# Forgetting attention and a GELU MLP on one core: key tiles joined on VectorE before the denominators, and the value weighting moved to another stage

## The chip, the cores and the metric

The kernel runs on one core of a Trainium2 chip. A core has five engines that run their own instruction streams: TensorE (PE, with its weight loads shown as PEld), VectorE (DVE), ScalarE (ACT), GpSimd (POOL) and SyncE (SP, here only a queue that issues transfers). GpSimd, SyncE and ScalarE issue DMAs from their own queues. The metric is the device time of one launch in microseconds: the median of the runs. Before the change it is 342.06 us (3 runs, 341.93 to 342.09).

## The reference

Eight batches with eight heads each, a sequence S of 576 and a head dimension of 64, then an MLP over the 4608 rows that the attention gives:

```python
scores = scale * np.matmul(q, k.transpose(0, 1, 3, 2))
cum = np.cumsum(np.log(np.clip(f, 0.0001, 1.0)), axis=-1)
decay = cum[:, :, :, None] - cum[:, :, None, :]
scores = np.where(causal, -1000000000.0, scores + decay)
attn = np.exp(scores - scores.max(axis=-1, keepdims=True))
attn = attn / (attn.sum(axis=-1, keepdims=True) + 1e-09)
x = np.matmul(attn, v)                        # then heads side by side: [4608, 512]
g = gelu_tanh(x @ w_in)                       # 512 -> 2048
out = g @ w_out                               # 2048 -> 512
```

The decay splits into a factor of the query, which cancels in the quotient, and a factor of the key. So with P = exp(scale * k q) under the causal mask and w[key] = exp(-cum[key] - 64), the output is (sum over keys of P w v) / (sum over keys of P w).

## The kernel before, in words

Work goes by quads: quad i is four heads of batch i // 2, so there are 16 quads. Keys lie on the partitions, five key tiles of 128 (the last holds 64). P of a quad is the tile `pt` [128, 4 heads, 1536 columns]; each head's columns are the pieces of L51: "low" (64 columns, the first 64 queries against the first keys), key tile 0 (512 columns), 1 (448), 2 (320), 3 (192) and "high", which shares the first 64 columns with "low" on the other partitions. A later key tile has fewer columns since the causal mask leaves fewer queries.

- `scores` (S, L202) makes P of a quad in three rounds: products on TensorE, exp on ScalarE (L228). `mask` (A in the new table, L230) then clears the triangle on GpSimd (`affine_select`, L234), in part also on VectorE (L263) for the early quads.
- `denominators` (D, L297) is the sum over keys of P w: `product` (L266) runs 24 matmuls, six pieces for four heads, with w as the weights; the four heads run side by side in 128x32 column groups of TensorE, so a piece costs its columns once. The result lies in the one PSUM buffer `psO`. VectorE then transposes, takes reciprocals and transposes back (L307 to L311).
- `attn_out` (V, L315) is the same product with `vw`, v times w, as the weights, for one half x of the head dimension; VectorE multiplies it by the reciprocals into `xT` (L319) and so frees `psO`.
- `make_vw` (VW, L174) computes v times w for a quad: one GpSimd instruction of 1280 elements a partition (L178). `copy_low` (CL, L182) copies a part of it on VectorE.
- `mlp_in` (L322) is the first MLP product for 512 rows (chunk c) with GELU, in eight parts of eight matmuls. `mlp_out` (L357) is the second, 64 units for a chunk; `out_part(c, n)` runs the next n units. Every 16 units VectorE copies a tile out (L373) and SP stores it.

The order is written out by hand, and all engines take their instructions in that order. SETUP and FRONT (L69 on) are tables of words for the first two chunks and the quads 0 to 6. From then on the main loop (L551 to L565) does for c = 2 to 8: the rest of `mlp_out` of chunk c-1, two parts of `mlp_in` of chunk c (the first MLP stage below), `prepare` (VectorE transposes the loaded k and q of quads 2c+3 and 2c+4, L161, and GpSimd issues the loads of k and q two quads ahead, L155), `load_v` of batch c+2 on SP's queue, the other six parts of `mlp_in`, six units of `mlp_out`, and `pair(2c+3, 2c+2, c)` (L524). A pair lays the scores of quad i = 2c+3 and of quad i+1 between the D and V of quad j = 2c+2 and of quad i, with units of `mlp_out` between all of these. Pairs run for c = 2 to 6, so they hold the D of quads 6 to 15. In the last pair there is no quad i+1.

After each round of scores `after_scores` (L517) issues the mask; after round 1 also `make_vw` of that quad on GpSimd, and after round 2 `copy_low` on VectorE.

Of the kernel before, what the change touches and what calls it, by code (L numbers as in the profile page):

```python
# [16 lines left out]
def kernel(  # L17
# [28 lines left out]
    CH = 512  # L46
    NCH = B * S // CH
    ZW = 64

    rounds = [(0, 512), (512, 512), (1024, 512)]  # L50
    pieces = [  # L51
# [28 lines left out]
        S.4.1 m.3.1 LQ.6 F.0.6 TQ.5 H.4.2.1 D.3 H.4.0.1 LQ.7 VW.4 H.4.0.0 V.3.1 v.3.0 f.0.3 H.4.2.0 CL.4 I.1.0 m.4.1 LV.2.1@LQ.5 I.1.5  # L80
        TQ.6 m.4.2.3 I.1.1 I.1.7 LV.3.0@LQ.7 m.4.2.2 TK.6 M.4.0 I.1.3 I.1.2 I.1.4 I.1.6 X F.1.8 S.5.0 F.1.2 F.1.14 S.5.1 D.4 M.5.0 f.1.9
        S.5.2 V.4.0 m.5.2.3 f.1.6 VW.5 V.4.1 CL.5 m.5.2.2 LQ.8 S.6.0 f.1.6 M.5.1 D.5 f.1.4 S.6.1 V.5.1 f.1.7 V.5.0 vw.6 S.6.2
        m.6.1 M.6.2.2 m.6.0 m.6.2.3 LK.7 LK.8 CL.6 LX.3.1@LK.6
    """

    singles = ctx.enter_context(tc.tile_pool(name="singles", bufs=1))
    ostage_pool = ctx.enter_context(tc.tile_pool(name="ostage", bufs=3))
# [5 lines left out]
    def many(n, shape, dtype, name):  # L93
        return [singles.tile(shape, dtype, name=f"{name}{i}") for i in range(n)]
# [19 lines left out]
    before = singles.tile([128, (NT - 1) * BH], FP32, name="before")  # L114
    wT = singles.tile([128, NQ, NT, 4], FP32, name="wT")
    w_bf = singles.tile([128, NQ, NT + 1, 4], BF16, name="w_bf")
    shift = singles.tile([128, 1], FP32, name="shift")
    idle = singles.tile([128, 512], BF16, name="idle")
    spare = singles.tile([1, 1], FP32, name="spare")
# [54 lines left out]
    def make_vw(i, eng, part=None):  # L174
        h0 = 4 * (i % QPB)
        vb = v_nat[(i // QPB) % 2]
        t0, t1 = {None: (0, NT), 0: (0, QA // 128), 1: (QA // 128, NT)}[part]
        eng.tensor_mul(  # L178
            vw[i % 2][:, t0:t1], vb[:, t0:t1, h0:h0 + 4, :],
            wT[:, i, t0:t1, :].unsqueeze(3).to_broadcast([128, t1 - t0, 4, D]))  # L180

    def copy_low(i):  # L182
        nc.vector.tensor_copy(vw[i % 2][64:128, LOW], vw[i % 2][0:64, 0])
# [18 lines left out]
    def scores(i, r, groups=((0, 1, 2, 3),)):  # L202

        qq, p = qT[i % 2], pt[i % 2]
        if i < 2:
            off, n = split_rounds[r]
            todo = [(key, col - off, q0, nq) for (key, col, q0, nq) in split_pieces[r]]
        else:
            off, n = rounds[r]
            todo = []  # L210
            for (key, col, q0, nq) in pieces:
                a, z = max(col, off), min(col + nq, off + n)
                if a < z:
                    todo.append((key, a - off, q0 + a - col, z - a))
        for heads in groups:
            tiles = {g: psS.tile([128, 2, 512], FP32, name="ps_s", tag="s") for g in sorted({h // 2 for h in heads})}
            for c in range(2):
                for j, (key, c0, q0, nq) in enumerate(todo):
                    for h in heads:
                        nc.tensor.matmul(  # L220
                            tiles[h // 2][:, h % 2, c0:c0 + nq],
                            key_columns(i, key, h, c),
                            qq[32 * h:32 * h + 32, q0:q0 + nq, c],
                            start=(c == 0 and j == 0), stop=(c == 1),
                            skip_group_check=True,
                        )
            for g, t in tiles.items():
                nc.scalar.activation(p[:, 2 * g:2 * g + 2, off:off + n], t[:, :, 0:n], AF.Exp, scale=scale)  # L228
# [37 lines left out]
    def product(i, groups, spare, part=None):  # L266
        p = pt[i % 2]
        if part is not None:
            s0, s1 = parts[part]
            po = psM.tile([128, 512], FP32, name="po_m", tag="m")  # L270
            for (key, col, q0, nq) in sorted(sum(split_pieces[1:] if part else split_pieces[:1], []), key=lambda x: HIGH if x[0] == "high" else x[0]):
                for (r0, lhsT, h) in groups:
                    w = lhsT(HIGH if key == "high" else key)
                    nc.tensor.matmul(  # L274
                        po[r0:r0 + w.shape[-1], q0 - s0:q0 - s0 + nq], w, p[:, h, col:col + nq],
                        start=(key == 0), stop=(key == (HIGH if part else 1)),
                        skip_group_check=True,
                    )
            return po[:, 0:s1 - s0]
        if spare:  # L280
            po = psS.tile([128, 2, 512], FP32, name="ps_o", tag="s").rearrange("p a n -> p (a n)")
        else:
            po = psO.tile([128, 1024], FP32, name="po", tag="po")
        for (key, col, q0, nq) in sorted(pieces, key=lambda x: {0: 0, "low": 1}.get(x[0], 2)):
            t = {"low": LOW, "high": HIGH}.get(key, key)
            for (r0, lhsT, h) in groups:
                w = lhsT(t)
                nc.tensor.matmul(  # L288
                    po[r0:r0 + w.shape[-1], 448 + q0:448 + q0 + nq], w, p[:, h, col:col + nq],
                    start=(key in (0, "low")), stop=(key in ("low", "high")),  # L290
                    skip_group_check=True,
                )
        return po[:, 448:448 + S]

    rbs = {}

    def denominators(i, part=None):  # L297

        def column(h):

            return lambda t: (w_bf[:, i, t, h:h + 1] if t not in (0, LOW) else
                              w_bf[:, i, t, h:h + 1].to_broadcast([128, 32]))

        po = product(i, [(32 * h, column(h), h) for h in range(4)], False, part)
        n = S if part is None else parts[part][1] - parts[part][0]
        den = den_pool.tile([128, S], FP32, name="den", tag="den")
        nc.vector.transpose(out=den[:, 0:n], in_=po)  # L307
        rec = den_pool.tile([128, S // 32], FP32, name="rec", tag="rec")
        nc.vector.reciprocal(rec[:, 0:n // 32], den[:, 0:n:32])
        rb = den_pool.tile([128, S], FP32, name="rb", tag="rb")  # L310
        nc.vector.transpose(out=rb[:, 0:n].rearrange("p (c j) -> p c j", j=32),  # L311
                            in_=rec[:, 0:n // 32].unsqueeze(2).to_broadcast([128, n // 32, 32]))
        rbs[i, part] = rb[:, 0:n]

    def attn_out(i, x, spare=False, part=None):  # L315
        b, u = i // QPB, i % QPB
        po = product(i, [(32 * h, lambda t, h=h: vw[i % 2][:, t, h, x:D:2], h) for h in range(4)], spare, part)
        s0, s1 = (0, S) if part is None else parts[part]
        nc.vector.tensor_mul(xT[:, 2 * u + x, S * b + s0:S * b + s1], po, rbs[i, part])  # L319
# [106 lines left out]
    def make_w():  # L426
# [3 lines left out]
        for (rows, t0, t1) in ((128, 0, HIGH), (64, HIGH, NT)):  # L430
# [2 lines left out]
                cum_ps[:rows, t0 * BH:t1 * BH].rearrange("p (t i h) -> p t i h", i=NQ, h=4),  # L433
                AF.Exp, scale=-1.0, bias=shift[:rows, :])

    by_columns = []

    def pull(it, n):
# [7 lines left out]
    def out_part(c, n, tiled=0):  # L446
        by_columns[:] = [True] * tiled
        pull(fills.setdefault(c, mlp_out(c)), n)
# [5 lines left out]
    def load_values(b, half):  # L454
# [33 lines left out]
        "F": out_part,  # L488
        "f": lambda c, n: out_part(c, n, 1),
        "B": keep_busy,  # L490
        "X": load_exp,
    }

# [8 lines left out]
                after(did[0], dmas[gate])  # L502
            dmas[word.replace("LP", "LU").replace("LX", "LV")] = did[-1]

    def beside(i, r, c, todo):

        if i is not None:
            scores(i, r)
        for n, x in enumerate(todo):
            if isinstance(x, int):  # L510
                out_part(c, x, 1)
            else:
                x()
            if n == 0 and i is not None:
                after_scores(i, r)

    def after_scores(i, r):  # L517
        mask(i, r)
        if r == 1:
            make_vw(i, nc.gpsimd)  # L520
        if r == 2:
            copy_low(i)

    def pair(i, j, c):  # L524

        D, V = (lambda q: lambda: denominators(q)), (lambda q, x, spare=False: lambda: attn_out(q, x, spare))
        beside(i, 0, c, [D(j), 12])
        beside(i, 1, c, [V(j, 0), 10])
        beside(i, 2, c, [V(j, 1), 9])
        if i + 1 < NQ:  # L530
            beside(i + 1, 0, c, [D(i), 10])
            beside(i + 1, 1, c, [V(i, 0), 5, V(i, 1), 4])
            scores(i + 1, 2)
            after_scores(i + 1, 2)
        else:
            beside(None, 0, c, [D(i), 10, V(i, 0), V(i, 1, True), 10])

    def prepare(*quads):

# [8 lines left out]
    with tc.manual_schedule():  # L548
        setup()
        run(FRONT)  # L550
        for c in range(2, NCH):  # L551
            out_part(c - 1, CH)
            for pr in range(2):
                mlp_in(c, (pr,))
            if c + 1 < B:
                prepare(2 * c + 3, 2 * c + 4)
            if c + 2 < B:
                load_v(c + 2)
            for pr in range(2, NP):
                mlp_in(c, (pr,))  # L560
            if c + 1 < B:
                load_exp()
                out_part(c, 6)
                pair(2 * c + 3, 2 * c + 2, c)
        out_part(NCH - 1, CH)  # L565
# [30 lines left out]
```

## Time and profile before

| what | value |
|---|---|
| median of the runs | 342.06 us (341.93 to 342.09) |
| profiled execution, span from first to last instruction | 339.9 us |
| TensorE clock granted in it | 1.000 |
| busy PE / ACT / DVE / POOL | 329.8 / 191.8 / 132.3 / 110.1 us |
| `denominators` product of one quad (po from w_bf, 24 matmuls) in the pairs | 0.69 us from its start to that of the next work |
| `make_vw` on GpSimd (L178), 1280 elements | 2.33 us each |

Times in timelines are microseconds from the start of the span: a line gives the start, the length, the engine, the line of the kernel, the operation with output and input, how many instructions are merged into the line, and in brackets how long the engine was idle before it and what released it. The part of a median run that lies outside the span is about 2.2 us.

### The profile page before, as it was taken

To read this page: it belongs to the slowest core of one execution; us is meant where nothing else is said; L and a number is where in the kernel's file an instruction comes from. 1 tells how busy PE (TensorE), PEld (TensorE's weight loads), DVE (VectorE), ACT (ScalarE), POOL (GpSimd) and SP (SyncE) were. 2 spreads that over 40 slices of the span, in tenths; PEclk is the share of its full clock that TensorE was granted. 3 is DMA by queue.
4 is the path that set the end of the run, shared out by engine and by line. 5 is a ranking of instruction groups with operands and counts; after the bars stand their busy time and mean duration, and the time that the engine had idled before them with its cause. 6 is when DMAs were issued, how large, how long until landed. Compare 5 with 4: busy or idle time off the path is not lost.

```text
span 339.9 us, 9423 instructions
## 1 busy us (share of the span) xinstructions
PE 329.8 (97%) x4241; PEld 162.0 (48%) x4241; DVE 132.3 (39%) x206; ACT 191.8 (56%) x201; POOL 110.1 (32%) x155
## 2 busy tenths in 40 slices
PE   3999999999999999999999999999999999999996
PEld 1458844544454445444444444444544454444443
DVE  4686059830465435703462244413430450021011
ACT  4784686677547665667566665674576624502510
POOL 8987551600506233601551145106410410000000
PEclk9999999999999999999999999999999999999999
DMA  7999999570316970591129210910100010011012
GB/s 127 207 216 214 196 230 194 102 172 2 95 36 101 227 156 33 131 205 39 35 77 207 59 67 35 212 30 35 63 31 2 33 63 34 2 62 62 0 40 85
DMA packets 40201, 33.26 MB, mean 98 GB/s; under 512 B 27473, under 2 KB 29777, under 8 KB 40161
## 3 DMA queue, kind: packets, MB, share of 16 engines
q0 software_dynamic: 8848, 16.58, 27.4%
q1 hardware_dynamic: 31168, 16.01, 17.0%
q8 instruction: 33, 0.54, 0.7%
q10 hardware_dynamic: 144, 0.07, 0.1%
q14 instruction: 8, 0.06, 0.0%
HBM read 36.85 MB, written 9.44 MB: 136 GB/s over the span
## 4 chain that ended last, share of the span: by engine, by line
PE 90%; DMA 2%; POOL 2%; ACT 2%; DVE 1%; issue 1%; POOLq 0%; DVEq 0%; ACTq 0%
PE pso L368 36%; PE ps_h L330 33%; PE po L288 8%; PE ps_s L220 8%; PE ps_h L347 4%; DMA v_nat<-in_v_dram 2%; ACT pt L228 2%; PE po_m L274 1%; POOL vw L178 1%; POOL v_nat L132 0%; PE ps_o L288 0%; DVE pt L263 0%; DVE vw L178 0%; POOL pt L234 0%; POOL q_c L155 0%
## 5 line engine op out<-in xcount | busy, mean ns | idle before, releaser
L368 PE MATMUL pso<-w_out_sb,gT 128*32 128x512 bf16 (+3 forms) x1492 | 134.5, 377 | 0.0
L228 ACT ACTIVATE pt<-ps_s 128x1024 bf16<-128x1024 f32 (+2 forms) x100 | 93.7, 988 | 53.6 <-PE ps_s L220 46.0
L330 PE MATMUL ps_h<-xT,w_in_sb 128*128 128x512 bf16 x512 | 111.9, 379 | 0.0
L337 ACT ACTIVATE gT<-ps_h 128x1024 bf16<-128x1024 f32 x64 | 65.5, 1024 | 64.1 <-PE ps_h L330 64.1
L234 POOL TENSOR_SCALAR_AFFINE_SELECT pt<-pt 128x512 bf16<-128x512 bf16 (+3 forms) x65 | 38.2, 597 | 140.6 <-ACT pt L228 139.7
L368 PEld LDWEIGHTS <-gT 128*32 128x32 bf16 (+1 forms) x1492 | 56.3, 97 | 56.8 <-issue 3.5
L330 PEld LDWEIGHTS <-w_in_sb 128*128 128x128 bf16 x512 | 50.0, 98 | 60.4 <-issue 0.4
L373 DVE COPY o_st<-pso 128x512 f32<-128x512 f32 (+2 forms) x37 | 24.9, 673 | 71.8 <-PE pso L368 71.5
L307 DVE STREAM_TRANSPOSE den<-po 128x576 f32<-128x576 f32 x14 | 11.0, 784 | 65.7 <-PE po L288 65.7
L220 PE MATMUL ps_s<-qT,kT 32*128 32x64 bf16 (+5 forms) x896 | 36.2, 264 | 0.2 <-ACT pt L228 0.2
L319 DVE TENSOR_TENSOR xT<-po,rb 128x576 bf16<-128x576 f32 x26 | 19.7, 757 | 31.6 <-PE po L288 31.5
L178 POOL TENSOR_TENSOR vw<-v_nat,wT 128x1280 bf16<-128x1280 f32 (+1 forms) x13 | 30.0, 2308 | 0.1
L220 PEld LDWEIGHTS <-kT 32*128 32x128 bf16 x896 | 16.4, 93 | 23.7 <-issue 18.8
L161 DVE STREAM_TRANSPOSE kT<-k_c 128x576 f32<-128x576 f32 x16 | 20.0, 1248 | 16.9 <-DMA k_c<-in_k_dram 16.8
L288 PE MATMUL po<-pt,vw 128*32 128x64 bf16 (+4 forms) x624 | 22.4, 278 | 0.0
L161 DVE STREAM_TRANSPOSE qT<-q_c 128x576 f32<-128x576 f32 x16 | 19.9, 1244 | 1.2 <-PE ps_s L220 0.7
L288 PEld LDWEIGHTS <-vw 128*32 128x32 bf16 x672 | 14.2, 97 | 11.8 <-issue 3.7
L132 POOL DMA_DIRECT2D v_nat<-in_v_dram x20 | 15.3, 776 | 3.4 <-DMA w_out_sb<-in_moe_w_out_dram 3.4
L347 PE MATMUL ps_h<-xT,w_in_sb 128*128 128x256 bf16 x128 | 14.5, 273 | 0.0
L347 PEld LDWEIGHTS <-w_in_sb 128*128 128x128 bf16 x128 | 12.3, 98 | 1.7
L311 DVE STREAM_TRANSPOSE rb<-rec 128x576 f32<-128x576 f32 (+2 forms) x18 | 12.8, 711 | 0.6
L155 POOL DMA_DIRECT2D k_c<-in_k_dram x16 | 9.1, 568 | 11.3 <-DVE kT L161 5.7
(61 smaller groups left out, 124.9 us busy)
## 6 DMA issues: line engine op xcount, KB each, us to landing
out_dram<-o_st SPq DMA_DIRECT2D x35, 256.0 KB, 2.1
k_c<-in_k_dram POOLq DMA_DIRECT2D x16, 288.0 KB, 6.8
q_c<-in_q_dram POOLq DMA_DIRECT2D x16, 288.0 KB, 7.4
v_nat<-in_v_dram SPq DMA_DIRECT2D x16, 256.0 KB, 8.3
w_in_sb<-in_moe_w_in_dram POOLq DMA_DIRECT2D x4, 512.0 KB, 9.5
w_out_sb<-in_moe_w_out_dram POOLq DMA_DIRECT2D x4, 512.0 KB, 7.2
v_nat<-in_v_dram SPq DMA_DIRECT2D x16, 128.0 KB, 3.3
v_nat<-in_v_dram POOLq DMA_DIRECT2D x13, 128.0 KB, 7.9
```

The source lines that it names most:

```text
L161: nc.vector.transpose(out=dst.rearrange("p s c -> p (s c)").bitcast(FP32) .rearrange("p (t a) -> p a t", a=S // 32), in_=src.rearrange("p ...
L178: eng.tensor_mul(vw[i % 2][:, t0:t1], vb[:, t0:t1, h0:h0 + 4, :], wT[:, i, t0:t1, :].unsqueeze(3).to_broadcast([128, t1 - t0, 4, D]))
L220: nc.tensor.matmul(tiles[h // 2][:, h % 2, c0:c0 + nq], key_columns(i, key, h, c), qq[32 * h:32 * h + 32, q0:q0 + nq, c], start=(c == 0 an ...
L228: nc.scalar.activation(p[:, 2 * g:2 * g + 2, off:off + n], t[:, :, 0:n], AF.Exp, scale=scale)
L234: nc.gpsimd.affine_select(out=x, in_=x, compare_op=ALU.is_ge, fill=0.0, base=0, pattern=pattern, channel_multiplier=-1)
L288: nc.tensor.matmul(po[r0:r0 + w.shape[-1], 448 + q0:448 + q0 + nq], w, p[:, h, col:col + nq], start=(key in (0, "low")), stop=(key in ("lo ...
L319: nc.vector.tensor_mul(xT[:, 2 * u + x, S * b + s0:S * b + s1], po, rbs[i, part])
L330: nc.tensor.matmul(ph[:, j, :], w_in_sb[:, dt, 128 * ft:128 * ft + 128], xT[:, dt, CH * c:CH * (c + 1)], start=(dt == 0), stop=(dt == N_DT ...
L337: nc.scalar.activation(gT[c % 2][:, 2 * pr:2 * pr + 2, :], ph, AF.Gelu_apprx_tanh)
L347: nc.tensor.matmul(ph[:, j // 2, QA * (j % 2):QA * (j % 2) + QA], w_in_sb[:, dt, 128 * ft:128 * ft + 128], xT[:, dt, n0:n0 + QA], start=(d ...
L368: nc.tensor.matmul(pso[c0:c0 + cols, m0:m1], gT[c % 2][:, ft, 128 * n + c0:128 * n + c0 + cols], w_out_sb[:, ft, m0:m1], start=(ft == 0), ...
L373: nc.vector.tensor_copy(st[:, m0:m1], pso[:, m0:m1])
```

## The change

For the quads from 6 on (FOLD = 6), VectorE first joins key tiles of P, so that the denominators' product has fewer columns to run. `fold_keys(i, t)` computes for each of four heads a = p_t * (w_t / w_t+1) + p_t+1 over the columns of key tile t+1 (448, 320 and 192 for t = 0, 1, 2). With a new table `ratio` of w_t / w_t+1, the sum of a * w_t+1 over the partitions is then that of both tiles. `folded_sums` takes the place of `product` in D: for a quad with all three levels the six pieces have 64, 64, 128, 128, 192 and 64 columns in place of 512, 64, 448, 320, 192 and 64 (640 for 1600 per head); for a quad with level 0 alone they have 64, 64, 448, 320, 192 and 64 (1152). All weights of it are broadcast to 32 columns (`wide`), where before this was so for two pieces.

The even quad j = 2c+2 of each pair gets all three levels, twelve VectorE instructions in the first MLP stage, after `prepare`. The odd quad i = 2c+3 gets level 0 alone, four instructions inside the pair (word E), behind the mask of its round 1. `make_vw` of both quads and `copy_low` move out of the pair: the first to the first MLP stage ahead of `prepare`, the second to behind the folds. `ratio` is made at the end of FRONT (RA), by a reciprocal and a product on VectorE.

```diff
@@ FRONT @@
-        m.6.1 M.6.2.2 m.6.0 m.6.2.3 LK.7 LK.8 CL.6 LX.3.1@LK.6
+        m.6.1 M.6.2.2 m.6.0 m.6.2.3 LK.7 LK.8 CL.6 LX.3.1@LK.6 RA
+    PAIR = """
+        S.i.0 D.j A.i.0 12 S.i.1 V.j.0 A.i.1 10 E.i.0 S.i.2 V.j.1 A.i.2 9
+        S.k.0 D.i A.k.0 10 S.k.1 V.i.0 A.k.1 5 V.i.1 4 S.k.2 A.k.2
+"""
+    LAST = """
+        S.i.0 D.j A.i.0 12 S.i.1 V.j.0 A.i.1 10 E.i.0 S.i.2 V.j.1 A.i.2 9
+        D.i 10 V.i.0 v.i.1 10
+"""
...
+    def fold_keys(i, t, heads=range(4)):
+        p, a = pt[i % 2], fold[i % 2]
+        q0, col = 128 * (t + 1), {0: 576, 1: 1024, 2: 1344}[t]
+        n = S - q0
+        for h in heads:
+            nc.vector.scalar_tensor_tensor(
+                a[:, h, q0 - 128:], p[:, h, 128:128 + n] if t == 0 else a[:, h, q0 - 128:],
+                ratio[:, i, t, h:h + 1], p[:, h, col:col + n], op0=ALU.mult, op1=ALU.add)
+        folded[i] = t + 1
+
+    def folded_sums(i, column, levels):
+        p, a = pt[i % 2], fold[i % 2]
+        po = psO.tile([128, 1024], FP32, name="po", tag="po")
+        todo = [(LOW, p[:, :, 0:64], 0), (0, p[:, :, 64:128], 64)]
+        for (t, q0, col, n) in ((1, 128, 576, 448), (2, 256, 1024, 320), (3, 384, 1344, 192)):
+            if t > levels:
+                todo.append((t, p[:, :, col:col + n], q0))
+            else:
+                z = S if t == levels else q0 + 128
+                todo.append((t, a[:, :, q0 - 128:z - 128], q0))
+        todo.append((HIGH, p[:, :, 0:64], 512))
+        for j, (t, x, q0) in enumerate(todo):
+            for h in range(4):
+                w = column(h)(t)
+                nc.tensor.matmul(
+                    po[32 * h:32 * h + w.shape[-1], 448 + q0:448 + q0 + x.shape[-1]], w, x[:, h, :],
+                    start=(j < 2), stop=(j in (0, len(todo) - 1)), skip_group_check=True)
+        return po[:, 448:448 + S]
...
+    def make_ratio():
+        r = ratio[:, FOLD:]
+        nc.vector.reciprocal(r, wT[:, FOLD:, 1:NT - 1, :])
+        nc.vector.tensor_mul(r, r, wT[:, FOLD:, 0:NT - 2, :])
...
     def after_scores(i, r):
         mask(i, r)
-        if r == 1:
-            make_vw(i, nc.gpsimd)
-        if r == 2:
-            copy_low(i)
...
             for pr in range(2):
                 mlp_in(c, (pr,))
             if c + 1 < B:
+                for i in (2 * c + 2, 2 * c + 3):
+                    if i > FOLD:
+                        make_vw(i, nc.gpsimd)
                 prepare(2 * c + 3, 2 * c + 4)
+                for t in range(3):
+                    fold_keys(2 * c + 2, t)
+                for i in (2 * c + 2, 2 * c + 3):
+                    if i > FOLD:
+                        copy_low(i)
             if c + 2 < B:
                 load_v(c + 2)
```

The tables PAIR and LAST hold the order that `pair` spelled out before, with E.i.0 as the one new word.

More of the change, by code (lines that the diff above doesn't have):

```diff
@@ L48 @@
     ZW = 64
+    FOLD = 6
     rounds = [(0, 512), (512, 512), (1024, 512)]
@@ L116 @@
     w_bf = singles.tile([128, NQ, NT + 1, 4], BF16, name="w_bf")
+    ratio = singles.tile([128, NQ, NT - 2, 4], FP32, name="ratio")
+    fold = many(2, [128, 4, S - 128], BF16, "fold")
     shift = singles.tile([128, 1], FP32, name="shift")
@@ L295 @@
     rbs = {}
+    folded = {}
+    def fold_keys(i, t, heads=range(4)):
[25 more added lines that the diff above has]
+        return po[:, 448:448 + S]
     def denominators(i, part=None):
+        wide = range(NT + 1) if i in folded else (0, LOW)
         def column(h):
-            return lambda t: (w_bf[:, i, t, h:h + 1] if t not in (0, LOW) else
+            return lambda t: (w_bf[:, i, t, h:h + 1] if t not in wide else
                               w_bf[:, i, t, h:h + 1].to_broadcast([128, 32]))
-        po = product(i, [(32 * h, column(h), h) for h in range(4)], False, part)
+        if i in folded:
+            po = folded_sums(i, column, folded[i])
+        else:
+            po = product(i, [(32 * h, column(h), h) for h in range(4)], False, part)
         n = S if part is None else parts[part][1] - parts[part][0]
@@ L490 @@
         "B": keep_busy,
+        "RA": make_ratio,
         "X": load_exp,
@@ L503, in run @@
             dmas[word.replace("LP", "LU").replace("LX", "LV")] = did[-1]
[L505 to L515, printed above, removed]
     def after_scores(i, r):
         mask(i, r)
-        if r == 1:
-            make_vw(i, nc.gpsimd)
-        if r == 2:
-            copy_low(i)
     def pair(i, j, c):
[L526 to L536, printed above, removed]
+        last = i + 1 == NQ
+        for word in (LAST if last else PAIR).split():
+            name, *args = word.split(".")
+            if name.isdigit():
+                out_part(c, int(name), 1)
+                continue
+            q, *args = args
+            q = {"i": i, "j": j, "k": i + 1}[q]
+            args = list(map(int, args))
+            if name == "A":
+                after_scores(q, *args)
+            elif name == "E":
+                fold_keys(q, args[0], args[1:] or range(4))
+            else:
+                ops[name](q, *args)
     def prepare(*quads):
```

## The prediction

> **What bounds it now.** I read the page's busy shares first, then the chain that ended last, then who TensorE waited for.
>
> ```profile
> PE 329.8 (97%) x4241; PEld 162.0 (48%) x4241; DVE 132.3 (39%) x206; ACT 191.8 (56%) x201; POOL 110.1 (32%) x155
> PEclk9999999999999999999999999999999999999999
> PE 90%; DMA 2%; POOL 2%; ACT 2%; DVE 1%; issue 1%; POOLq 0%; DVEq 0%; ACTq 0%
> PE ps_lt L402 <- ACT f_sb L397: 4.8, 1, 4.8
> PE cum_ps L429 <- POOL before L422: 1.0, 1, 1.0
> ```
>
> TensorE is 97% busy at a granted clock of 1.000, makes 90% of the chain, and its named waits lie in the start-up. So from the first pair on, a column less on TensorE is time, unless a new wait eats it, and an added VectorE instruction costs nothing until TensorE has to wait for it.
>
> **What the shorter products save.** The third view is the timeline around one D:
>
> ```profile
> 155.01 0.86 PE L288 MATMUL po<-pt,w_bf 128*32 128x512 bf16 x24
> 155.70 2.76 PE L368 MATMUL pso<-w_out_sb,gT 128*32 128x512 bf16 x48
> ```
>
> From start to start a D takes 0.69 us. Its single matmuls in the trace start in groups of four, 226 ns after the first group of 512 columns, then 28 (64), 190 (448), 136 (320), 82 (192) and 29 (64): sum 691. A piece thus costs its columns at about 0.42 ns and 2 ns more; 128 columns, which no D has, I take at 56, between 28 and 82. A fully folded D is 28+28+56+56+82+29 plus the 10 ns by which the first group runs over its columns: 289, a gain of 0.40. With level 0 alone it is 28+28+190+136+82+29+10 = 503, a gain of 0.19. The wider weights cost nothing: V's groups have 32-column weights throughout, and its 64-column group also gives way after 29 ns.
>
> Ten D's change. One gains nothing, the last one:
>
> ```profile
> 272.42 1.23 POOL L234 TENSOR_SCALAR_AFFINE_SELECT pt<-pt 128x512 bf16<-128x512 bf16 x2 [0.55 <-ACT pt L228]
> 272.86 1.12 PE L288 MATMUL po<-pt,w_bf 128*32 128x512 bf16 x24
> 273.81 2.33 PE L368 MATMUL pso<-w_out_sb,gT 128*32 128x512 bf16 x40
> ```
>
> It already takes 0.95: its 192-column group waits for the second select, which ends at 273.65 behind ScalarE's exp, not behind `make_vw`, which ended at 271.87. A shorter D only waits longer. So 5 x 0.40 + 4 x 0.19 = 2.76 us.
>
> **What the folds cost VectorE.** No row has this operation. Below it lies L263, two bf16 operands of 512: the second of them starts 0.336 behind the first (103.17, 103.50). Above it among products lies L178 on VectorE with fp32: 512 elements every 0.605 (14.71, a pair lasting 1.29 whose last takes 0.684) and 1280 in 1.40 (101.77 to 103.17), which gives 1.035 ns an element and 75 ns an instruction. The far upper end are the transposes of L161, 576 in 1.09, 1.76 ns an element by the same 75. A fold multiplies by an fp32 scalar and adds; every row with an fp32 operand runs near one element a cycle, only the pure bf16 one is faster. I take the middle: 540, 406 and 274 ns for 448, 320 and 192, so twelve take 4.87 us (ends 2.86 and 7.66) and four take 2.15 (ends 1.2 and 3.5).
>
> The Trainium skill, "Vector Engine (DVE) Microarchitecture Reference", section 5.1, lists the operations for which faster modes are enabled: copy, cast, tensor_scalar and tensor_tensor. The joined multiply and add is not among them, so by the page the bf16 row is no guide: by it the total below is 341.15, by the bf16 row 339.3.
>
> **GpSimd beside VectorE.** These rows show that the two collide:
>
> ```profile
> 23.24 0.94 DVE L178 TENSOR_TENSOR vw<-v_nat,wT 128x768 bf16<-128x768 f32 x1
> 23.49 2.03 POOL L178 TENSOR_TENSOR vw<-v_nat,wT 128x768 bf16<-128x768 f32 x1
> 103.17 1.52 DVE L263 TENSOR_TENSOR pt<-pt,causal 128x512 bf16<-128x512 bf16 x3
> 103.69 0.72 POOL L234 TENSOR_SCALAR_AFFINE_SELECT pt<-pt 128x512 bf16<-128x512 bf16 x1 [13.16 <-ACT pt L228]
> ```
>
> 768 elements at the 2.33/1280 of an undisturbed GpSimd `make_vw` would be 1.40; it took 2.03 and was late by the rest of the VectorE product in front of it. The third L263 began in the middle of the select and took 0.85 where its neighbours took 0.42: it lost 0.43 of the select's 0.72. The transposes of L161 took 1.25 beside a `make_vw` (32.11) as elsewhere. So one `make_vw` that falls among the folds costs them 2.33 less some 0.25, as 0.29 hid in starting up there: 2.1 us; least 0, most 2.33.
>
> The rule speaks against this change: "SBUF — State Buffer", section "Who interferes with whom", has an instruction of VectorE with two SBUF inputs and a GpSimd one that reads SBUF exclude each other for a whole instruction. By it the loss is 2.33 and the total 341.4; by the row 2.1 and 341.15.
>
> **Where the folds are in time, and where not.** In the stages c = 3 to 6 they are. At c = 3 the selects end at 140.83 and two `make_vw` at 145.5; the transposes leave VectorE at 144.33; 1.2 lost and 4.87 of folds end near 150.4, and D starts at 155.01, 4.6 to spare (4.5 at c = 6, with two transposes alone). Without that cover every microsecond late is one on the path. At c = 2 it is gone:
>
> ```profile
> 105.44 3.66 POOL L132 DMA_DIRECT2D v_nat<-in_v_dram  x5
> 109.36 1.26 DVE L161 STREAM_TRANSPOSE kT<-k_c 128x576 f32<-128x576 f32 x1 [3.69 <-DMA k_c<-in_k_dram]
> 110.91 0.55 POOL L155 DMA_DIRECT2D k_c<-in_k_dram  x1 [1.81 <-DVE kT L161]
> 112.89 1.23 DVE L161 STREAM_TRANSPOSE qT<-q_c 128x576 f32<-128x576 f32 x1
> 119.09 0.87 PE L288 MATMUL po<-pt,w_bf 128*32 128x512 bf16 x24
> ```
>
> Here VectorE waits for k, so its transposes end at 112.89+1.09 = 113.98, and the folds of quad 6 at 118.85. D wants the last of them at 119.09+0.17 = 119.26: in time by 0.4. But `make_vw(7)` now stands in this stage, and its values come with the five transfers at 105.44; the last, issued at 108.4, takes 7.6, so it starts near 116.0, among the folds. They end at 118.85+2.1 = 120.95, and with 0.15 to reach TensorE the stall is 1.85 us (least 0, most 3.0 with the transfer issues behind it in the way too). Behind that D stands all of TensorE's queue. 2 us without matmuls showed no lower clock before (4.8 us of waiting above, clock 1.000).
>
> **Parts at nothing.** The four folds inside a pair start after the mask (161.83 at c = 3) and end at 164.0; the product of V that frees `psO` slips from 163.40 to 164.0 and ends at 164.8, D needs `psO` at 165.85. In the last pair it is 272.6 against 272.86. Dearer folds would stall here next. Leaving the pair, `make_vw` and `copy_low` free nothing: the selects waited for ScalarE (0.55 idle). The loads of k and q are now behind `make_vw` on GpSimd's queue: issued from 118.4 instead of 110.91 at c = 2, landed 7.4 later, about 128, needed at 139.99; at c = 3 from 145.5, needed at 175.9. If that gap closed, the transposes would wait. SP's `load_v` follows readers that now finish earlier. RA: reciprocals of 18 and 8 elements take 267 and 203 ns, so 120 take 0.9, with a product 1.1, between 104.95 and the idle 3.69 before 109.36; a copy, its store and `load_v(4)` behind it start 1.1 later, and those values are not read before 140.8.
>
> **Sum.** On the profiled span, 339.9-2.76+1.85 = 339.0; the part outside is 2.2, so on the median 342.06-0.91 = 341.15.
>
> **The rivals.**
> 1. No stall at c = 2: the folds run as fast as the bf16 row (113.98+2.86+2.1 = 118.95), or GpSimd gives way until they end. For: operands are bf16. Against: the fp32 scalar, and the select that went in between two L263. 342.06-2.76 = 339.3; chance 0.18.
> 2. Slower, folds too dear: at the 1.76 ns of the transposes twelve take 7.66 and end at 123.8, a stall of 4.6; four take 3.5, `psO` is late by 0.4 in four pairs and about 1.0 in the last, 2.6 in all: 342.06-2.76+4.6+2.6 = 346.5. It decides from 5.8 us for the twelve on, where the c = 2 stall alone is the 2.76. For: one operand is read through a second path. Against: all products stand near 1.04 ns. Chance 0.12.
> 3. The product doesn't get shorter: short groups are held by four weight loads at the 97 ns mean of their row, so a folded D takes 0.58 and gains 0.11, the other, held at its three short groups and the one of 192, nothing; with the stall 342.06-0.55+1.75 = 343.3. Against: 64-column groups that give way after 28 ns. Chance 0.05.
>
> The forecast has 0.65. Its own range is 340.4 to 342.0 (50 ns a fold either way, and the GpSimd loss 1.8 to 2.33). The range 339.1 to 342.7 takes in rival 1 and the upper bound of the stall, and leaves out rivals 2 and 3. A measurement tells 0.2% (0.7 us) from no change: the forecast falls below 341.38 with about 0.65 of its chance and else almost all within; with rival 1 faster is 0.60, same 0.20, and slower 0.20 with rivals 2, 3 and the forecast's tail.
>
> **What would show it.** D rows of w_bf starting 0.29 and 0.50 before their neighbours; folds of 448 near 0.54 apart; one fold of quad 6 lengthened to over 2 us beside `make_vw` near 116; TensorE waiting for VectorE near 119 once and at no later D. Wrong it is if that wait is missing or comes back at every pair, or if folds of 448 take 0.3 or 0.9.

## The result and the profile after

The changed kernel takes 340.58 us (median of 6 runs, 339.88 to 341.28) where the kernel before takes 341.85 beside it (6 runs, 341.43 to 342.09): a ratio of 0.9972, 95% interval 0.9961 to 0.9982, so 0.6 to 1.3 us faster. On a later run of the same kernel the ratio was 0.9967 (0.9946 to 0.9989). The profiled execution has a span of 339.2 us, 0.7 less than that of before.

The first view is the page of the changed kernel: busy time and its share, and the engines' work in it.

```profile
PE 326.2 (96%) x4219; PEld 162.3 (48%) x4241; DVE 179.7 (53%) x288; ACT 191.7 (57%) x201; POOL 110.8 (33%) x155
```

VectorE is busy for 47 us more, its waits for GpSimd among them, and TensorE for 3.6 less, of which some is matmuls that the trace misses (4219 of 4241 are there). The next view is the timeline of the changed kernel around the D of an even and of an odd quad in the stage c = 3; its lines are numbered anew, L337 is the product in `folded_sums`, L418 that of `mlp_out`, L317 the fold.

```profile
156.45 0.24 PE L337 MATMUL po<-pt,w_bf 128*32 128x64 bf16 x8
156.74 2.76 PE L418 MATMUL pso<-w_out_sb,gT 128*32 128x512 bf16 x48
162.90 2.47 DVE L317 SCALAR_TENSOR_TENSOR fold<-pt,ratio 128x448 bf16<-128x448 bf16 x4 [1.22 <-POOL pt L247]
165.29 0.75 DVE L369 TENSOR_TENSOR xT<-po,rb 128x576 bf16<-128x576 f32 x1
166.89 0.24 PE L337 MATMUL po<-pt,w_bf 128*32 128x64 bf16 x8
167.40 2.33 PE L418 MATMUL pso<-w_out_sb,gT 128*32 128x512 bf16 x40
```

An even D gives way after 0.29 us, an odd one after 0.51; both took 0.69. The four folds of the odd quad and V's multiplication behind them end at 166.04, ahead of the D at 166.89. The same view at c = 2:

```profile
113.64 2.38 DVE L317 SCALAR_TENSOR_TENSOR fold<-pt,ratio 128x448 bf16<-128x448 bf16 x4
115.94 5.32 DVE L317 SCALAR_TENSOR_TENSOR fold<-fold,ratio,pt 128x320 bf16<-128x320 bf16 x8
115.98 2.70 POOL L191 TENSOR_TENSOR vw<-v_nat,wT 128x1280 bf16<-128x1280 f32 x1 [6.94 <-DMA v_nat<-in_v_dram]
119.05 0.24 PE L337 MATMUL po<-pt,w_bf 128*32 128x64 bf16 x8
120.00 1.56 PE L337 MATMUL po<-fold,w_bf 128*32 128x128 bf16 x5 [0.24 <-DVE fold L317]
121.43 2.75 PE L418 MATMUL pso<-w_out_sb,gT 128*32 128x512 bf16 x45
```

Here the D takes 2.38 from start to start, 2.1 longer than at c = 3. `make_vw(7)` begins at 115.98, among the folds: of the eight folds from 115.94 on, the second starts at 116.41 and the next only 2.54 us later, where folds of this size follow each other every 0.46. The view of VectorE between 116.5 and 118.8 holds that fold alone:

```profile
116.41 2.62 DVE L317 SCALAR_TENSOR_TENSOR fold<-fold,ratio,pt 128x320 bf16<-128x320 bf16 x1
```

TensorE takes up the heads one by one as their folds come. The list of TensorE's waits shows almost nothing of it, since the wait is cut into pieces and the modelled ends of the matmuls cover most of each:

```profile
PE po L337 <- DVE fold L317: 0.2, 1, 0.2
```

The stages tell it best. Between the first matmul of one first MLP stage and that of the next, all traces of this study have the same lengths wherever their order of work is the same, to 0.03 us. What differs from run to run lies before the stage c = 2 (its start column) and in how that stage meets its transfers. The part after the stage c = 6 took 58.8 us in each.

| kernel | start | c = 2 | c = 3, 4, 5 each | c = 6 |
|---|---|---|---|---|
| before | 103.27 | 35.91 | 35.91 | 34.19 |
| changed | 103.22 | 37.41 | 35.33 | 33.79 |
| changed, again | 103.30 | 37.70 | 35.33 | 33.80 |
| e1_vw7_later | 103.65 | 35.63 | 35.33 | 33.80 |
| e2_folds_first | 102.84 | 35.32 | 35.33 | 33.79 |
| e3_move_alone | 103.12 | 35.91 | 35.91 | 34.18 |
| e4_folds_alone | 103.53 | 37.50 | 37.35 | 37.54 |
| e5_short_no_folds | 103.80 | 35.33 | 35.33 | 33.80 |
| e6_no_fold_15 | 103.01 | 35.33 | 35.33 | 33.79 |
| e7_even_only | 103.59 | 35.51 | 35.51 | 33.79 |
| e8_last_later | 103.27 | 35.32 | 35.33 | 33.37 |
| e9_write_then_read | 102.75 | 37.35 | 35.33 | 33.80 |

So the change gives 0.58 in each of three stages and 0.40 in the last, and loses 1.50 at c = 2. The start column differs by up to 1.05 us; what lies behind that is in the last section.

### The profile page after: what moved, and what is told of

Read it like the earlier page. It is cut to its first block, busy times and chain, and to the rows that moved or that the text cites. A ratio compares the mean times of both kernels' runs of the same rounds, so it can differ in the third digit from the quotient of the medians.

```text
span 339.2 us, 9512 instructions
## 1 busy us (share of the span) xinstructions
PE 326.2 (96%) x4219; PEld 162.3 (48%) x4241; DVE 179.7 (53%) x288; ACT 191.7 (57%) x201; POOL 110.8 (33%) x155
## 4 chain that ended last, share of the span: by engine, by line
PE 75%; issue 12%; POOL 4%; DVE 4%; ACT 2%; DMA 1%; POOLq 0%; ACTq 0%
PE pso L418 31%; PE ps_h L380 24%; PE ps_s L233 7%; PE po L301 5%; PE ps_h L397 4%; DVE fold L317 2%; ACT pt L241 2%; POOL pt L247 1%; DMA k_c<-in_k_dram 1%; PE po_m L287 1%; PE po L337 1%; PE idle_ps L212 1%; DVE kT L174 1%; POOL v_nat L145 1%; POOL vw L191 1%
## 5 line engine op out<-in xcount | busy, mean ns | idle before, releaser
L418 PE MATMUL pso<-w_out_sb,gT 128*32 128x512 bf16 (+2 forms) x1479 | 132.4, 377 | 1.6 <-issue 1.4
L418 PEld LDWEIGHTS <-gT 128*32 128x32 bf16 (+1 forms) x1492 | 57.1, 97 | 56.0 <-issue 3.5
L380 PEld LDWEIGHTS <-w_in_sb 128*128 128x128 bf16 x512 | 50.0, 98 | 60.5 <-issue 0.4
L317 DVE SCALAR_TENSOR_TENSOR fold<-pt,ratio 128x448 bf16<-128x448 bf16 x40 | 30.4, 821 | 6.1 <-POOL pt L247 6.1
L301 PEld LDWEIGHTS <-vw 128*32 128x32 bf16 x672 | 14.3, 97 | 11.8 <-issue 3.7
L317 DVE SCALAR_TENSOR_TENSOR fold<-fold,ratio,pt 128x320 bf16<-128x320 bf16 (+1 forms) x40 | 18.3, 525 | 0.0
L361 DVE STREAM_TRANSPOSE rb<-rec 128x576 f32<-128x576 f32 (+2 forms) x18 | 12.8, 712 | 0.6
```

Of the source, the lines that this page charges most:

```text
L301: nc.tensor.matmul(po[r0:r0 + w.shape[-1], 448 + q0:448 + q0 + nq], w, p[:, h, col:col + nq], start=(key in (0, "low")), stop=(key in ("lo ...
L317: nc.vector.scalar_tensor_tensor(a[:, h, q0 - 128:], p[:, h, 128:128 + n] if t == 0 else a[:, h, q0 - 128:], ratio[:, i, t, h:h + 1], p[:, ...
L380: nc.tensor.matmul(ph[:, j, :], w_in_sb[:, dt, 128 * ft:128 * ft + 128], xT[:, dt, CH * c:CH * (c + 1)], start=(dt == 0), stop=(dt == N_DT ...
L418: nc.tensor.matmul(pso[c0:c0 + cols, m0:m1], gT[c % 2][:, ft, 128 * n + c0:128 * n + c0 + cols], w_out_sb[:, ft, m0:m1], start=(ft == 0), ...
```

## The experiments

**Is it the one GpSimd instruction?** The theory was that the folds of quad 6 are late because `make_vw(7)` falls among them. The rivals: the folds are too slow for that stage anyway (A), or the gain comes from moving work out of the pairs (B). The first kernel, e1, moves `make_vw(7)` alone (and its `copy_low`):

```diff
                 for i in (2 * c + 2, 2 * c + 3):
-                    if i > FOLD:
+                    if i > FOLD + 1:
                         make_vw(i, nc.gpsimd)
...
     def after_scores(i, r):
         mask(i, r)
+        if i == FOLD + 1 and r == 0:
+            make_vw(i, nc.gpsimd)
+        if i == FOLD + 1 and r == 1:
+            copy_low(i)
```

> Only GpSimd's v times w of quad 7 leaves the stage at c = 2, for behind the mask of round 0 of its pair; nothing else moves. Theory (the folds of quad 6 are late because that one GpSimd instruction falls among them): the wait of TensorE near 119 shrinks from 2.1 us to 0 to 0.2, and the time falls to about 2.7 us below the kernel before (339.2 against 341.85). Rival A (the twelve folds are too slow for that stage by themselves): the wait stays near 2 us and the time that of the changed kernel, 340.6. Rival B (the gain comes from moving work out of the pairs, the shorter products give nothing): no difference to the changed kernel.

It took 339.18 us, before 341.55 beside it: 0.9933 (0.9921 to 0.9946). Its timeline at c = 2:

```profile
114.36 2.39 DVE L317 SCALAR_TENSOR_TENSOR fold<-pt,ratio 128x448 bf16<-128x448 bf16 x4
116.66 3.25 DVE L317 SCALAR_TENSOR_TENSOR fold<-fold,ratio,pt 128x320 bf16<-128x320 bf16 x8
119.47 0.24 PE L337 MATMUL po<-pt,w_bf 128*32 128x64 bf16 x8
120.08 1.24 PE L418 MATMUL pso<-w_out_sb,gT 128*32 128x512 bf16 x17
```

The eight folds take 3.25 in place of 5.32, and the wait is 0.3 (stage 35.63 against 35.33), a little over the 0.2 expected. B falls, and A as the reason for 2 us. But the folds have no slack of their own either: the transposes ended 10.71 after the start of the stage, 0.3 later than in the changed kernel's profile (10.42), and the wait is as long. The second profiled execution of the changed kernel, at the end of this section, had its transposes over after 10.72 and took 37.70 for this stage, so at the same landing of k the one GpSimd instruction costs 2.07.

**Can the folds stand where VectorE is idle?** The second kernel, e2, moves the folds at c = 2:

```diff
+                for t in range(3 if c == 2 else 0):
+                    fold_keys(2 * c + 2, t)
                 prepare(2 * c + 3, 2 * c + 4)
-                for t in range(3):
+                for t in range(3 if c > 2 else 0):
                     fold_keys(2 * c + 2, t)
```

> At c = 2 alone the twelve folds of quad 6 stand ahead of VectorE's transposes, in the 2.4 us in which it waits for k; they end near 112.5, before the values of quad 7 have landed. Theory: no wait near 119 at all, transposes over by 117, 2.8 us below the kernel before (339.1). Rival A expects the same here, so that it is told from the theory by the run with the later v times w. Rival B: as the changed kernel, 340.6. A third way it could go: the transposes of quad 7 end too late for its scores at 118.4, then a wait at the scores takes the place of the old one.

It took 338.58 us, before 341.55: 0.9916 (0.9902 to 0.9929). Timeline at c = 2, with the last eight of the twelve folds in its first line:

```profile
108.64 3.25 DVE L317 SCALAR_TENSOR_TENSOR fold<-fold,ratio,pt 128x320 bf16<-128x320 bf16 x8
111.81 1.25 DVE L174 STREAM_TRANSPOSE kT<-k_c 128x576 f32<-128x576 f32 x1
115.32 2.33 POOL L191 TENSOR_TENSOR vw<-v_nat,wT 128x1280 bf16<-128x1280 f32 x1 [6.66 <-DVE kT L174]
118.67 0.24 PE L337 MATMUL po<-pt,w_bf 128*32 128x64 bf16 x8
118.96 1.25 PE L418 MATMUL pso<-w_out_sb,gT 128*32 128x512 bf16 x20
```

The D takes 0.29 here too, and `make_vw(7)`, now beside a transpose, its usual 2.33. No new wait at the scores. The stage has the length of the others.

**Does moving alone bring anything?** In e3 the folds and the E of both tables are left out, the old product stays:

```diff
-        S.i.0 D.j A.i.0 12 S.i.1 V.j.0 A.i.1 10 E.i.0 S.i.2 V.j.1 A.i.2 9
+        S.i.0 D.j A.i.0 12 S.i.1 V.j.0 A.i.1 10 S.i.2 V.j.1 A.i.2 9
...
-                for t in range(3):
-                    fold_keys(2 * c + 2, t)
```

> No folds and the old denominators; v times w and its copy stay moved into the first MLP stage. Theory: nothing in the pairs waited for them, so the time is that of the kernel before within 0.2 us. Rival B: the whole gain of the changed kernel, 1.3 us below before or more.

It took 341.44 us against 341.55, 0.9999 (0.9990 to 1.0007), and all stages as before. Moving is worth nothing by itself, and with it goes what is left of rival B.

**Is it needed for the folds?** The other half alone, e4:

```diff
-                for i in (2 * c + 2, 2 * c + 3):
-                    if i > FOLD:
-                        make_vw(i, nc.gpsimd)
...
     def after_scores(i, r):
         mask(i, r)
+        if r == 1:
+            make_vw(i, nc.gpsimd)
+        if r == 2:
+            copy_low(i)
```

> Folds and short denominators, but v times w and its copy stay in the pairs, behind the mask of round 1, which is where the four folds of the odd quad start. Theory (the two exclude each other): those folds lose 2.1 us, V's multiplication behind them frees its accumulator 1.3 us too late for the next D in four pairs and about 1.6 in the last one; at c = 2 the folds of quad 6 are in time to 0.2 us. In sum -2.8 + 5.2 + 1.6 + 0.1 = 4.1 us above the kernel before. Rival (VectorE and GpSimd only slow each other a little there): 2 us below the kernel before or more.

It took 351.89 us against 341.55: 1.0305 (1.0286 to 1.0325), 10.3 us slower. The direction was right, the size was not: 4.1 had been expected. Timeline of the stage c = 3, with TensorE's wait in the last brackets, and the list of waits:

```profile
163.25 2.33 POOL L191 TENSOR_TENSOR vw<-v_nat,wT 128x1280 bf16<-128x1280 f32 x1
163.31 5.29 DVE L317 SCALAR_TENSOR_TENSOR fold<-pt,ratio 128x448 bf16<-128x448 bf16 x4 [1.22 <-POOL pt L247]
166.12 2.00 POOL L247 TENSOR_SCALAR_AFFINE_SELECT pt<-pt 128x512 bf16<-128x512 bf16 x2 [0.55 <-ACT pt L241]
168.52 0.74 DVE L369 TENSOR_TENSOR xT<-po,rb 128x576 bf16<-128x576 f32 x1
169.32 0.24 PE L337 MATMUL po<-pt,w_bf 128*32 128x64 bf16 x8 [1.96 <-DVE xT L369]
...
PE po L337 <- DVE xT L369: 10.4, 5, 2.6
```

The four folds take 5.29 in place of 2.47. They lose to `make_vw`, and then to the two selects that follow, which themselves take 2.00 for 1.23: the second collision was left out of the expectation. V's multiplication is late, `psO` with it: of the 2.82 lost the changed kernel's 0.85 to spare covers a part, and D waits 1.96 in four pairs. In the last pair it waits 2.57 and more is lost behind it, as the last section shows.

**What do the folds cost TensorE?** In e5 `folded_sums` reads P itself and no fold is made, so the sums lack the joined tiles:

```diff
-        for h in heads:
-            nc.vector.scalar_tensor_tensor(
-                a[:, h, q0 - 128:], p[:, h, 128:128 + n] if t == 0 else a[:, h, q0 - 128:],
-                ratio[:, i, t, h:h + 1], p[:, h, col:col + n], op0=ALU.mult, op1=ALU.add)
...
-                todo.append((t, a[:, :, q0 - 128:z - 128], q0))
+                todo.append((t, p[:, :, q0 - 128:z - 128], q0))
```

> The version with the folds of quad 6 ahead of the transposes, but without any fold: the short denominators read P itself where they would read the joined tile, so the sums lack the joined key tiles. It is TensorE's part of the change alone. Theory: the folds lie wholly beside TensorE in that version, so the time is the same, 3.0 us below the kernel before, within 0.3. Rival: 200 more VectorE instructions cost TensorE something in passing (waits of single matmuls on folds, buffers that come free later), then this one is faster by 0.5 us or more.

It took 339.19 us, before 341.71 beside it: 0.9908 (0.9873 to 0.9943). Four of its six runs lie at 339.0 to 339.4 and two at 338.4 to 338.5. That is 0.6 above e2 by the medians, more than the 0.3 expected, but not in the part that the folds touch: every stage is as long as in e2, and the profiled run's start is the latest of the table, 0.96 behind that of e2. So the rival falls: the folds cost TensorE nothing where they are done ahead of their D.

**Which D's bring it?** Two kernels on top of e2: no E in the last pair (e6, the edit in LAST alone), and no E at all (e7, the same edit in PAIR and LAST).

```diff
-        S.i.0 D.j A.i.0 12 S.i.1 V.j.0 A.i.1 10 E.i.0 S.i.2 V.j.1 A.i.2 9
+        S.i.0 D.j A.i.0 12 S.i.1 V.j.0 A.i.1 10 S.i.2 V.j.1 A.i.2 9
```

> The version with the folds of quad 6 first, without the fold of quad 15, whose denominators are long again. Theory: that D waits for the last select anyway, so the time is the same within 0.2 us, 3.0 below the kernel before, and the wait in its middle falls from 0.45 to 0.26 us. Rival: every shorter D is worth its columns, then 0.2 us slower.

> The version with the folds of quad 6 first, without the folds inside the pairs: only the even quads are joined. Theory: the odd quads gave 4 x 0.18 = 0.7 us, so 2.2 to 2.3 us below the kernel before. Rival: the four folds inside a pair cost as much as they bring (the multiplication behind them is late), then the same or faster than with them.

Without the fold of quad 15: 338.57 us, 0.9904 (0.9870 to 0.9938), the last stage 33.79 as with it. That D gains nothing from being shorter: its group of 192 columns waits 0.26 for the select where with the fold it waits 0.45. Even quads alone: 339.62 us, 0.9924 (0.9898 to 0.9951); the stages are 35.51, 0.18 longer in four of them, which is the 0.7 expected (the medians say 1.0, with starts of 103.59 and 102.84 in the profiles).

**And if the last D starts later?** On top of e2, in e8, two units of `mlp_out` change sides:

```diff
-        S.i.0 D.j A.i.0 12 S.i.1 V.j.0 A.i.1 10 E.i.0 S.i.2 V.j.1 A.i.2 9
-        D.i 10 V.i.0 v.i.1 10
+        S.i.0 D.j A.i.0 12 S.i.1 V.j.0 A.i.1 10 E.i.0 S.i.2 V.j.1 A.i.2 11
+        D.i 8 V.i.0 v.i.1 10
```

> The version with the folds of quad 6 first; in the last pair two of the ten units of the second MLP product that stand behind the D of quad 15 stand ahead of it, so that the last select is over when it starts. Theory: its wait of 0.45 us goes and nothing takes its place, 3.4 us below the kernel before. Rival: with eight units behind it the reciprocals come too late for V, and the wait moves there: 3.0 us below before or less.

It took 338.33 us, before 341.71: 0.9886 (0.9848 to 0.9923). The timeline of e2 at this D, then that of this kernel:

```profile
269.93 0.32 PE L337 MATMUL po<-pt,w_bf 128*32 128x320 bf16 x4
270.51 0.29 PE L337 MATMUL po<-pt,w_bf 128*32 128x192 bf16 x8 [0.27 <-POOL pt L247]
```

```profile
270.79 0.45 PE L337 MATMUL po<-pt,w_bf 128*32 128x320 bf16 x12
271.05 1.91 PE L418 MATMUL pso<-w_out_sb,gT 128*32 128x512 bf16 x32
```

In e2 the group of 192 columns began 0.58 behind that of 320, 0.45 more than the columns take; now the product runs through, and the last stage is 0.42 shorter with nothing in its place. This is the fastest of these versions: 3.4 us below the kernel before.

**What of GpSimd shuts the folds out?** On top of e1, at c = 2, with two new tiles `scratch` of 640 elements a partition (e9):

```diff
                 prepare(2 * c + 3, 2 * c + 4)
+                if c == 2:
+                    nc.gpsimd.memset(scratch[0], 0.0)
+                    nc.gpsimd.memset(scratch[1], 0.0)
+                    nc.gpsimd.tensor_copy(scratch[1], scratch[0])
+                    nc.gpsimd.tensor_copy(scratch[0], scratch[1])
```

> The version with the later v times w of quad 7; in its place GpSimd has two instructions that only write (memset of 640 elements) and two that read and write (copies of 640) behind the transposes at c = 2, all of them beside the folds of quad 6. Theory: it is GpSimd's reading that shuts out a product with two SBUF operands, so the folds beside the memsets keep their distance of 0.46 to 0.6 us and those beside the copies lose the copies' length less some 0.3. Rival (any GpSimd access does it): the folds beside the memsets lose as much. Second rival (it is the two-operand v times w alone): none loses anything.

It took 340.34 us in its one run. The next are timelines of VectorE and of GpSimd in this kernel; it has a line more ahead of the fold, so that is L318:

```profile
115.37 1.28 DVE L318 SCALAR_TENSOR_TENSOR fold<-pt,ratio 128x448 bf16<-128x448 bf16 x2
116.55 1.95 DVE L318 SCALAR_TENSOR_TENSOR fold<-fold,ratio,pt 128x320 bf16<-128x320 bf16 x2
...
115.23 0.65 POOL L611 MEMSET scratch<- 128x640 bf16 x1
115.80 0.65 POOL L612 MEMSET scratch<- 128x640 bf16 x1
116.52 0.72 POOL L613 COPY scratch<-scratch 128x640 bf16<-128x640 bf16 x1
117.30 0.86 POOL L614 COPY scratch<-scratch 128x640 bf16<-128x640 bf16 x1
```

The two folds of 448 beside the memsets took 115.37 to 116.55, 0.59 each, their undisturbed distance. The two of 320 beside the copies started 0.95 and 0.92 ahead of what followed, where 0.46 is usual: 0.49 and 0.46 lost to copies of 0.72 and 0.86. In this execution reading does it and writing alone does not, so both rivals fall. The stage took 37.35 all the same, 2.02 over the others: the transposes ended 11.51 after its start, 1.09 later than in the changed kernel's profile, and the copies add 0.94.

**The changed kernel again.**

> The changed kernel once more, on the chip and in the rounds of this call. Theory: the same stage lengths as in its first profile (35.33 us, and 37.4 at c = 2), about 0.7 to 1.3 us below the kernel before by the medians; the start-up before the first of these stages differs by some tenths from run to run.

It took 340.73 us (339.74 to 341.73, 12 runs), before 341.57. The stage c = 2 was 37.70: its transposes ended 0.4 later (114.02), and so did all behind them. The size of that wait thus follows the landing of k: the transposes ended 10.72 after the start of the stage in place of 10.42, and the stage is as much longer.

## Why the prediction was right, point by point

- **TensorE is the bound, and columns are time.** Right. The D's gain 0.40 and 0.19 as predicted (0.18 by the stages of e7) and the last none; the five stages of e2 sum to 4 x 0.58 + 0.40 = 2.7 us of gain, 2.76 predicted, and its median is 3.0 lower (2.4 to 3.3).
- **The price of a fold.** The choice between the rows was right, the size a bit low. Folds follow each other every 596, 463 and 329 ns for 448, 320 and 192 elements: 1.05 ns an element as predicted, but 130 ns an instruction in place of the 75 taken from the products of `make_vw`. Twelve take 5.55 us, not 4.87. The bf16 row, which would have given rival 1, was no guide. The list of operations with faster modes in the Trainium skill, "Vector Engine (DVE) Microarchitecture Reference", section 5.1, from which this one is missing, agrees with the measured 1.05 ns.
- **GpSimd beside VectorE.** Right. The predicted loss was 2.1, the fold that met `make_vw(7)` lost 2.54-0.46 = 2.08. What is lost is the other instruction's length less 0.25; beside the copies of e9 it is the length less 0.23 and less 0.40. The Trainium skill, "SBUF — State Buffer", section "Who interferes with whom", would have had the whole 2.33; it also has GpSimd instructions that only write leave such products alone, which the memsets of e9 show.
- **Where the folds are late.** Right: at c = 2 alone, by 2.1 us, 1.85 predicted. Two misses cancel in part, folds 0.7 dearer and transposes 0.35 earlier (113.64, not 113.98). That the sum came so near was luck there: of the 0.4 that the folds were said to have to spare without the collision nothing was left, and in e1, where k came 0.3 later, they were late by 0.3 without it. At c = 3 to 6 the folds lose time as well and hide it (at c = 3 they end at 152.30, D starts at 156.45), since e2 has the same lengths there as e5 without folds.
- **Parts at nothing.** Moving `make_vw` and `copy_low` frees nothing (e3). The loads of k, issued later as said, are still in time: the transposes at c = 3 start at 141.43 without a wait. The folds inside the pairs are in time, by 0.85 at c = 3; with that cover gone (e4) the price was 2.0 a pair, so this part rests on the move.
- **The sum.** Span 339.9-2.7+2.1 = 339.3, measured 339.2, predicted 339.0. The median fell by 1.3 where 0.9 was forecast; the profile's 0.7 and the interval's 0.6 to 1.3 hold both. The remainder is the start-up, which moved by up to a microsecond between traces, whatever the kernel. One term was mis-sized: the part outside the span is not 2.2, which set a median beside the span of another execution. Every run on record that has both shows 1.6 to 1.8 (340.9 and 339.2 in the changed kernel's profiled one), and 339.0 with 1.7 is 340.7, near the 340.58. The measured 340.58 lies between the 341.15 forecast and the 339.3 of rival 1; what tells these two apart is the stage at c = 2, 2.1 longer than the others.
- **What went wrong.** In the prediction, the 2.2 above and the reading of the clock behind the 4.8 us of waiting, which the last section takes up. Neither touches the forecast gain, the second by luck: the clock did stay at 1.00 in the wait at c = 2. Behind it, the expectation for e4: of the two collisions inside the pair only the first was priced.

## What to carry to other kernels

Work given to an idle engine to relieve the bound one is free only where it is done in time at its tightest stage, so find the stage with the least slack, here the only one in which VectorE still waits for a transfer, and price that one. When two engines shut each other out, look for the place in which the idle engine waits for something else: the same twelve instructions cost 2.1 us behind the transposes and nothing ahead of them. And measure by stages where the order is fixed: lengths that agree to 0.03 us settle what medians with a spread of one microsecond leave open.

## What was not expected of the hardware

In the profiled execution of e4 the last wait of TensorE, 2.57 us, was followed by a lower granted clock, the four of 1.96 us were not. The view is that of busy time by stretches of e4; PEclk is the third number from the end of a line.

```profile
131.00:133.00 2.00, 1.03 (x36) 0.70 (x40) 1.94 (x5) 1.04 (x2) 0.83 (x2) 1.00 0.00 0
281.35:283.00 1.65, 1.65 (x32) 0.93 (x36) 1.33 (x3) 0.00 (x0) 0.00 (x0) 0.50 0.00 0
283.00:284.50 1.50, 1.50 (x20) 0.57 (x16) 1.39 (x3) 0.00 (x0) 0.00 (x0) 0.55 0.47 175
284.50:286.00 1.50, 1.50 (x40) 0.73 (x32) 0.00 (x0) 0.00 (x0) 0.00 (x0) 1.00 0.00 0
```

For about 3 us behind the wait, from its end at 281.35 on, the clock stood at half, which is most of why the last stage of e4 lost 3.75 us and not 2.1, the 2.57 less the 0.45 that this D waits in e2 anyway. The four runs of e4 have mean clocks of 0.995 and 0.990, and the two at 0.990 are the slower ones (352.83 and 352.31 us against 351.07 and 351.47), so the profiled execution is not the worst of them. The changed kernel's own wait of 2.1 us, in pieces with matmuls between them, showed 1.00 throughout.

The prediction had read from 4.8 us of waiting in the start-up that a wait of this length leaves the clock alone. That row cannot show it: the trace of before has no record of the clock ahead of 12.8 us, and the views count that as 1.00. The matmuls themselves ran at half pace there. The first two lines are timelines of before, the third of e5:

```profile
10.55 2.00 PE L199 MATMUL idle_ps<-idle 128*128 128x384 bf16 x6
13.00 0.66 PE L199 MATMUL idle_ps<-idle 128*128 128x384 bf16 x3
13.30 1.14 PE L212 MATMUL idle_ps<-idle 128*128 128x384 bf16 x3
```

Matmuls of 384 columns start every 0.32 us at 11.2 to 11.8, and every 0.16 at 13.2; in e5 they are still 0.32 apart at 13.6 to 13.9. The first record of the clock at 1.00 lies between 12.1 us (e9) and 15.2 us (e5), and these two have the earliest and the latest start in the table of stages, 102.75 and 103.80. One and the same matmul of the start-up begins at 14.11 in e9 and at 15.13 in e5, so 1.02 of the 1.05 between them arises here. What ends the half pace sooner or later, no run here shows.
